# Turned reads issued from SyncE, a gate in fifteen steps, one-hot pairs in two

## The chip, the cores and the metric

The kernel runs on one core of one Trainium2 chip. The metric is the device time of one execution in microseconds (us). The core has five engines that each take their own instructions in order: TensorE (PE, the matmuls), VectorE (DVE), ScalarE (ACT), GpSimd (POOL) and SyncE (SP, which here only issues DMAs). A DMA can be issued from several of them; the issuing instruction stands in that engine's queue with its wait.

## The reference

Three stages follow each other: a long convolution by FFT of 8 sequences of 3072 tokens with 256 channels, a mixture of eight experts with a capacity, and a dense layer pair with softplus.

```python
X = np.fft.rfft(x, axis=1)                       # x: 8 x 3072 x 256
y = np.fft.irfft(X * (filt_r + 1j * filt_i)[None], n=3072, axis=1)
x = y.reshape(8 * 3072, 256)

logits = x @ w_gate                              # 8 experts
expert = argmax(logits, axis=1)
gate = softmax(logits)[n, expert]                # sum + 1e-9 below
pos[i] = how many tokens before i chose the same expert
keep[i] = pos[i] < capacity                      # capacity 3072 // 8 * 2 = 768
y = relu(x @ w1[expert]) @ w2[expert]            # 256 -> 1024 -> 256
x = gate * y where keep, else 0

g = softplus(x @ w_in)                           # 256 -> 2048
return g @ w_out                                 # 2048 -> 256
```

With these inputs the capacity is used up early: the first three sequences (STATIC = 3) fill every expert, and all later tokens get the same constant row. A flag that the kernel computes guards a second, general path (from line 1200 on).

## The kernel before

**Stages.** For a sequence ("batch" b = 0, 1, 2) the FFT is split into 96 x 32. Batch 0 takes its first transform channel by channel and is turned on TensorE. Batches 1 and 2 do it with `x1_out` on TensorE and `x1_s` on ScalarE, then `store_mid` writes the rows to the DRAM tensor `mid` and `load_i` reads them back turned, twelve reads of 256 KB a batch. Both are issued from ScalarE's queue. A read needs all eight stores of its batch and one of four buffers "it". Then, for k from 0 to 11: `s2` (TensorE, two k at a time, three PSUM buffers "y"), `times_f` (VectorE, three instructions, called the filter product here), `z_sum` (GpSimd, one addition), `s3` (TensorE) and `s3_e` (ScalarE). When all twelve are done, `gsum`, `gturn` and the gate run on one side, and on the other `tr2`, `s4`, `s4_y` and `park` bring the sequence back to time order, scaled by the gate weight, and store it to `rowsd`; batches 0 and 1 are stored from SP, batch 2 from ScalarE.

**Gate and tables.** `gate` (line 437) is a generator; each `yield` ends a node of the plan. It takes the maximum, the exponential, the gate weight `ga`, then the first expert with the maximum (`v`, `vm`, `oh`), the rank among the tokens of the batch (`rk`, a scan, and a small matmul `pb` over partitions) and from it a slot number, which is split into 7 low bits and a block number in `ij`. `table_d` (line 496) makes two one-hot tensors of four tokens a piece, `lo` with 96x512 elements and `hv` with 96x192; `table_h` multiplies `hv` by the token number on GpSimd; `table_p` multiplies the pair on TensorE; `table_s` sums. Eight pieces (q) make a batch's table of which token stands in which slot. `table_end` and `slot_index` turn it into indices for the gather.

**Experts.** A unit is one expert and 384 slots; there are 16. `load_x` gathers its rows by three indirect DMAs from GpSimd, then `tr_p` turns them, `w1_p` and `w2_p` multiply in split precision (a high and a low part of each operand), `wi` and `wo` do the second pair of layers with softplus between on ScalarE, VectorE and GpSimd. The weights of the second pair arrive as 64-bit numbers and are taken apart by sixteen conversions (`split_res`, lines 614 to 633): five VectorE instructions, two of ScalarE and one of GpSimd each. Those that the plan places keep an intermediate in PSUM (`pv`); those placed after the plan's end keep it in SBUF (`wv`).

**Order.** Until the third unit's first matmuls the order on all engines comes from the class `Plan`, a list scheduler that runs when the program is built. Each node has an engine, a cost in ns, what it comes after (`after`), which ring of buffers it takes and gives, and `lock` where the node is to be planned as exclusive with the other locked nodes of VectorE and GpSimd. A node is chosen by its earliest start and, among equals, by the longest way to the end, to which `LIFT` adds a value for groups of nodes. A DMA is a node of its queue's engine with cost 70. What is left of the conversions when the plan's last TensorE node ends is placed in a fixed pattern of steps, which issues the other thirteen units.

The gate's slot number before:

```python
nc.vector.tensor_tensor(out=q, in0=rk, in1=eoff..., op=ALU.add)          # 96x256
nc.vector.tensor_scalar(ov, rk, cap + 0.5, float(OOB), op0=ALU.is_gt, op1=ALU.mult)
nc.vector.tensor_tensor(out=q, in0=q, in1=ov, op=ALU.add)
nc.vector.tensor_tensor(out=q, in0=q, in1=oh, op=ALU.mult)
nc.vector.tensor_reduce(out=ixf, in_=q.rearrange("p e n -> p n e"), axis=AXL.X, op=ALU.add)
```

Of the kernel before, what the change touches and what calls it, by code (L numbers as in the profile page):

```python
# [7 lines left out]
F32 = mybir.dt.float32  # L8
# [4 lines left out]
ALU = mybir.AluOpType  # L13
# [4 lines left out]
NB, S, D, E = 8, 3072, 256, 8  # L18
FF, DFF = 1024, 2048
NT = NB * S  # L20
N1, N2 = 96, 32
# [74 lines left out]
class Plan:  # L96
# [5 lines left out]
    LIFT = {"c_1": 64533380, "c_2": 22634, "left": 5719228183, "t_0": 111954045036084720, "t_1": 12832497819,  # L102
            "t_2": 63738405, "w1_2": 74362, "xl_1": 53055670, "yh_0": 108904, "yl_1": 70586}
# [13 lines left out]
    def order(self, lift):  # L117
# [45 lines left out]
        while ready:  # L163
# [19 lines left out]
            if nbytes:  # L183
                bus = max(bus, t + cost + 1200) + nbytes / 285
                done[n] = bus + 600
# [12 lines left out]
def body(tc, cap, x, ff, fx, wg, w1, w2, win, wout, m1, m2, m3, m4, small, out):  # L198
# [26 lines left out]
    eoff = sm[0:N1, 584:592]  # L225
# [16 lines left out]
    class Conv:  # L242
# [88 lines left out]
        def load_i(self, b, k):  # L331

            self.it[b, k] = self.ip.tile([128, 2, D], F32, name="it", tag="it")
            nc.scalar.dma_start(self.it[b, k], mid[b - 1].rearrange("(p k) c -> k p c", k=128)[:, 2 * k:2 * k + 2])
# [102 lines left out]
        def gate(self, b):  # L437
# [17 lines left out]
            nc.vector.tensor_reduce(out=sx, in_=ex, axis=AXL.X, op=ALU.add)  # L455
            nc.vector.tensor_scalar(sx, sx, 1e-9, None, op0=ALU.add)
# [4 lines left out]
            nc.vector.scalar_tensor_tensor(out=v, in0=dl, scalar=0.0, in1=wexp, op0=ALU.is_equal, op1=ALU.mult)  # L461
            vm = gp.tile([N1, N2], F32, name="vm")
            nc.vector.tensor_reduce(out=vm, in_=v, axis=AXL.X, op=ALU.max)
            oh = gp.tile([N1, E, N2], F32, name="oh", tag="ex")
            nc.vector.tensor_tensor(out=oh.rearrange("p e n -> p n e"), in0=v,
                                    in1=vm.unsqueeze(2).to_broadcast([N1, N2, E]), op=ALU.is_equal)
            rk = gp.tile([N1, E, N2], F32, name="rk")
            nc.vector.tensor_tensor_scan(
                out=rk.rearrange("p e n -> p (e n)"), data0=resetm, data1=oh.rearrange("p e n -> p (e n)"),
                initial=0.0, op0=ALU.mult, op1=ALU.add)  # L470
            cn = gp.tile([N1, E], F32, name="cn")
# [7 lines left out]
            nc.vector.tensor_tensor(out=ctot, in0=ctot, in1=cn, op=ALU.add)  # L479
            yield  # L480
            ov = dl.rearrange("p n e -> p (n e)").rearrange("p (e n) -> p e n", n=N2)
            q = v.rearrange("p n e -> p (n e)").rearrange("p (e n) -> p e n", n=N2)
            nc.vector.tensor_tensor(out=q, in0=rk, in1=eoff.unsqueeze(2).to_broadcast([N1, E, N2]), op=ALU.add)
            nc.vector.tensor_scalar(ov, rk, cap + 0.5, float(OOB), op0=ALU.is_gt, op1=ALU.mult)
            nc.vector.tensor_tensor(out=q, in0=q, in1=ov, op=ALU.add)
            nc.vector.tensor_tensor(out=q, in0=q, in1=oh, op=ALU.mult)
            ixf = gp.tile([N1, N2], F32, name="ixf")
            nc.vector.tensor_reduce(out=ixf, in_=q.rearrange("p e n -> p n e"), axis=AXL.X, op=ALU.add)
            yield
# [853 lines left out]
```

## Time and profile before

| | |
|---|---|
| time, three runs | 1083.91 us median, 1082.23 to 1084.74 |
| the profiled execution | 1082.4 us, span 1080.5 us, 19041 instructions |
| TensorE busy | 1035.3 us, 96% of the span |
| ScalarE busy | 778.2 us, 72% |
| GpSimd busy | 605.0 us, 56% |
| VectorE busy | 496.9 us, 46% |
| mean granted clock of TensorE | 0.984 |

The busy times are means over stages of different kinds. The convolutions, gates and tables of the three batches and the first units lie in the first 330 us; after that a pattern of 16 steps a unit repeats. A busy TensorE is not TensorE at its peak: its matmuls are pipelined and their ends are modelled, and at a granted clock of 0.5 the same matmul is busy twice as long. Idle time in front of an instruction is put down to what came last before it started.

### The profile page before, as it was taken

The numbers are of one execution on the slowest core, as the hardware profiler recorded it, in microseconds if no ns is written. First come the engines' busy times: TensorE is split into PE (matmuls) and PEld (weight loads), VectorE is DVE, ScalarE is ACT, GpSimd is POOL, SyncE is SP. The second block draws the span as 40 slices with busy tenths as digits, with TensorE's granted clock in tenths as the row PEclk, the third lists the DMA queues.
The fourth block names the chain that finished last, engine by engine and source line by source line (L and its number), as shares of the span: only waits on it lengthen the run. The fifth ranks groups of instructions, "written<-read, shape, count | busy, mean of one in ns | idle before, by whom it ended". The sixth has DMA issues, their size and how long they took to land.

```text
span 1080.5 us, 19041 instructions
## 1 busy us (share of the span) xinstructions
PE 1035.3 (96%) x7112; PEld 958.2 (89%) x7112; DVE 496.9 (46%) x884; ACT 778.2 (72%) x1612; POOL 605.0 (56%) x560
## 2 busy tenths in 40 slices
PE   8999999898899999999999999999999999999994
PEld 7656656598799999999999999999999999999994
DVE  3869699797866533333333333333333332323221
ACT  4554657665787877777877787777878777878882
POOL 0514244585765565856666656666575757463553
PEclk9999999898999999999999999999999999999997
DMA  9977526653311364323233332332121212100000
GB/s 290 290 237 258 168 79 190 200 183 108 105 40 54 117 216 165 128 103 126 94 113 114 120 114 94 113 115 66 49 70 39 70 49 69 32 15 1 16 15 18
DMA packets 72821, 120.02 MB, mean 111 GB/s; under 512 B 6928, under 2 KB 46736, under 8 KB 72720
## 3 DMA queue, kind: packets, MB, share of 16 engines
q1 hardware_dynamic: 58896, 90.40, 26.2%
q10 hardware_dynamic: 9216, 15.73, 4.5%
q0 software_dynamic: 4608, 12.59, 3.3%
q8 instruction: 58, 0.95, 0.4%
q14 instruction: 43, 0.35, 0.1%
HBM read 71.51 MB, written 47.19 MB: 110 GB/s over the span
## 4 chain that ended last, share of the span: by engine, by line
PE 79%; DVE 9%; DMA 4%; ACT 2%; issue 2%; POOL 2%; ACTq 0%; POOLq 0%; DVEq 0%; SPq 0%
PE po L803 23%; PE pi L779 23%; PE pw L725 11%; PE py L754 11%; PE p L425 2%; PE p L320 2%; PE p L297 1%; DVE hv L503 1%; DMA xt<-in_x_dram 1%; PE p L386 1%; POOL gl L554 1%; DMA fi<-in_fx_dram 1%; PE p L373 1%; DVE lo L503 1%; PE pt L702 1%
## 5 line engine op out<-in xcount | busy, mean ns | idle before, releaser
L645 DVE SCALAR_TENSOR_TENSOR g<-pi,ln 128x384 f32<-128x384 f32 x256 | 142.7, 557 | 494.4 <-ACT ln L640 433.3
L554 POOL TENSOR_TENSOR gl<-g,gh 128x384 fp32r<-128x384 f32 x256 | 262.2, 1028 | 116.8 <-ACT gh L553 115.2
L803 PE MATMUL po<-woh,gh 128*128 128x256 f32 x768 | 216.8, 282 | 3.5 <-DVE ot L810 3.5
L803 PE MATMUL po<-woh,gl 128*128 128x256 f32 x768 | 216.7, 282 | 0.0
L803 PE MATMUL po<-wol,gh 128*128 128x256 f32 x768 | 216.3, 282 | 0.0
L637 ACT ACTIVATE ab<-pi 128x384 f32<-128x384 f32 x256 | 124.7, 487 | 126.9 <-PE pi L779 120.8
L779 PE MATMUL pi<-yh,wih 128*128 128x384 f32 x512 | 173.6, 339 | 7.7 <-DVE g L645 7.7
L779 PE MATMUL pi<-yh,wil 128*128 128x384 f32 x512 | 173.8, 340 | 0.0
L779 PE MATMUL pi<-yl,wih 128*128 128x384 f32 x512 | 173.6, 339 | 0.0
L677 POOL TENSOR_TENSOR w1l<-ws,w1h 128x512 fp32r<-128x512 f32 x64 | 84.7, 1324 | 124.9 <-ACT w1h L672 95.8
L803 PEld LDWEIGHTS po<-woh,gh 128*128 128x128 f32 x768 | 144.3, 188 | 6.1 <-ACT ab L637 2.5
L803 PEld LDWEIGHTS po<-wol,gh 128*128 128x128 f32 x768 | 145.4, 189 | 0.0
L803 PEld LDWEIGHTS po<-woh,gl 128*128 128x128 f32 x768 | 145.0, 189 | 0.0
L638 ACT ACTIVATE ab<-ab 128x384 f32<-128x384 f32 (+1 forms) x257 | 134.9, 525 | 8.4
L640 ACT ACTIVATE ln<-ab 128x384 f32<-128x384 f32 (+1 forms) x257 | 134.6, 524 | 8.3
L553 ACT CAST gh<-g 128x384 fp32r<-128x384 f32 x256 | 130.4, 509 | 0.3 <-DVE g L645 0.3
L677 POOL TENSOR_TENSOR w2l<-ws,w2h 128x512 fp32r<-128x512 f32 x64 | 84.1, 1314 | 56.3 <-ACT w2h L672 55.1
L779 PEld LDWEIGHTS pi<-yh,wih 128*128 128x128 f32 x512 | 96.7, 189 | 9.1 <-DVE g L645 9.1
L779 PEld LDWEIGHTS pi<-yl,wih 128*128 128x128 f32 x512 | 96.8, 189 | 0.0
L779 PEld LDWEIGHTS pi<-yh,wil 128*128 128x128 f32 x512 | 96.7, 189 | 0.0
L365 POOL TENSOR_TENSOR z<-z,t 128x512 f32<-128x512 f32 x36 | 48.4, 1346 | 86.0 <-DVE t L360 78.6
L754 PE MATMUL py<-hl,w2h 128*128 128x384 f32 x256 | 86.2, 337 | 4.3 <-DVE hl L737 4.3
(145 smaller groups left out, 1942.9 us busy)
## 6 DMA issues: line engine op xcount, KB each, us to landing
ws<-in_w_dram SPq DMA_DIRECT2D x128, 256.0 KB, 2.9
out_dram<-cs SPq DMA_DIRECT2D x48, 512.0 KB, 3.9
xt<-in_x_dram SPq DMA_DIRECT2D x24, 384.0 KB, 7.1
mid<-s ACTq DMA_DIRECT2D x16, 384.0 KB, 4.9
rowsd<-yt SPq DMA_DIRECT2D x16, 384.0 KB, 3.2
it<-mid ACTq DMA_DIRECT2D x24, 256.0 KB, 3.9
wst<-in_win_dram SPq DMA_DIRECT2D x8, 512.0 KB, 4.5
wst<-in_wout_dram SPq DMA_DIRECT2D x8, 512.0 KB, 3.5
```

The costliest lines, as they stand in the source:

```text
L365: nc.gpsimd.tensor_tensor(out=z, in0=z, in1=t2, op=ALU.add)
L553: nc.scalar.copy(dst_hi, src)
L554: nc.gpsimd.tensor_tensor(out=dst_lo, in0=src, in1=dst_hi.bitcast(F32), op=ALU.subtract)
L637: nc.scalar.activation(out=ab[:, :n], in_=h, func=ACTF.Abs)
L638: nc.scalar.activation(out=ab[:, :n], in_=ab[:, :n], func=ACTF.Exp, scale=-1.0)
L640: nc.scalar.activation(out=ln[:, :n], in_=ab[:, :n], func=ACTF.Ln, bias=1.0)
L645: nc.vector.scalar_tensor_tensor(out=g[:, :n], in0=h, scalar=0.0, in1=ln[:, :n], op0=ALU.max, op1=ALU.add)
L677: nc.gpsimd.tensor_tensor(out=lo, in0=self.ws.pop(i), in1=hi.bitcast(F32), op=ALU.subtract)
L725: nc.tensor.matmul(ps, lhsT=a[:, k, fs], rhs=b[:, k], start=(n == 0), stop=(n == 5))
L754: nc.tensor.matmul(self.py[d], lhsT=a[:, j % 2, ds], rhs=b, start=(j == 0 and n == 0), stop=(j == 7 and n == 2))
L779: nc.tensor.matmul(self.pi, lhsT=a[i // 2][:, i % 2, k], rhs=b[:, k], start=(n == 0), stop=(n == 5))
L803: nc.tensor.matmul(self.po[t], lhsT=a[:, ts], rhs=b[:, i], skip_group_check=True, start=(i == 0 and n == 0 and t != 1), stop=(i == KI - 1 ...
```

## The change

Six things change, all in the planned part and in the gate that both paths share.

1. `load_i` issues its DMA from SP, and its node is planned on SP.
2. The gate yields more often: fifteen nodes G(0) to G(14) where there were nine.
3. The slot number is formed after the sum over experts. The expert's offset comes from `vm` (`eo`, 96x32), and the compare with the capacity and the two additions work on 96x32 instead of 96x256. The addition to `ctot` moves behind.
4. `table_d` makes one of the two one-hot tensors per call, and the pair is two nodes, `tl` and `tv`.
5. The end of a table and the making of the indices are two nodes.
6. The plan has new costs, `lock` marks and `LIFT` values, and a store of turned rows counts as landed 4000 ns after its bytes instead of 600.

```diff
@@ -99,8 +99,10 @@
 
     BUFS = {"a": 3, "y": 3, "o": 2, "it": 4, "z": 3, "t2": 2, "j": 4, "yt": 3, "xt": 8, "s1": 3, "e0": 1, "e1": 1,
             "gx": 1, "gsb": 1, "lo": 2, "wst": 3, "wf": 2, "ws": 5, "w1h": 3, "w2h": 3, "xd": 3, "x": 2, "h": 4, "Y": 3}
-    LIFT = {"c_1": 64533380, "c_2": 22634, "left": 5719228183, "t_0": 111954045036084720, "t_1": 12832497819,
-            "t_2": 63738405, "w1_2": 74362, "xl_1": 53055670, "yh_0": 108904, "yl_1": 70586}
+    LIFT = {"c_13": 153297, "c_5": 84850, "hl_1": 301914, "left": 201045, "s4_2": 324143,
+            "t_0": 6101450062220531419740490261209376882688, "t_1": 415592, "t_2": 383997, "tr2_2": 397489,
+            "xh_2": 208350, "yh_0": 307360}
+    MID = 4000
     HOP = {"PE": 250, "ACT": 130, "DVE": 130, "POOL": 100, "SP": 0}
 
     def __init__(self):
@@ -182,7 +184,7 @@
                 port = t + cost
             if nbytes:
                 bus = max(bus, t + cost + 1200) + nbytes / 285
-                done[n] = bus + 600
+                done[n] = bus + (self.MID if n[0] == "mid" else 600)
             for i, tag in enumerate(take):
                 rings[tag].append((n, take[:i].count(tag)))
             out.append(n)
@@ -222,7 +224,6 @@
     ones = sm[0:N1, 224:320]
     resetm = sm[0:N1, 320:576]
     wexp = sm[0:N1, 576:584].unsqueeze(1).to_broadcast([N1, N2, E])
-    eoff = sm[0:N1, 584:592]
     tok1 = sm[0:N1, 592:624]
     iota = sm[0:N1, 624:]
     ctot = const.tile([N1, E], F32, name="ctot")
@@ -331,7 +332,7 @@
         def load_i(self, b, k):
 
             self.it[b, k] = self.ip.tile([128, 2, D], F32, name="it", tag="it")
-            nc.scalar.dma_start(self.it[b, k], mid[b - 1].rearrange("(p k) c -> k p c", k=128)[:, 2 * k:2 * k + 2])
+            nc.sync.dma_start(self.it[b, k], mid[b - 1].rearrange("(p k) c -> k p c", k=128)[:, 2 * k:2 * k + 2])
 
         def s2(self, b, kk):
 
@@ -453,21 +454,28 @@
             yield
             sx = gp.tile([N1, N2], F32, name="sx")
             nc.vector.tensor_reduce(out=sx, in_=ex, axis=AXL.X, op=ALU.add)
+            yield
             nc.vector.tensor_scalar(sx, sx, 1e-9, None, op0=ALU.add)
             self.ga[b] = gp.tile([N1, N2], F32, name="ga", tag="ga", bufs=2)
             nc.vector.reciprocal(out=self.ga[b], in_=sx)
             yield
             v = gp.tile([N1, N2, E], F32, name="v")
             nc.vector.scalar_tensor_tensor(out=v, in0=dl, scalar=0.0, in1=wexp, op0=ALU.is_equal, op1=ALU.mult)
+            yield
             vm = gp.tile([N1, N2], F32, name="vm")
             nc.vector.tensor_reduce(out=vm, in_=v, axis=AXL.X, op=ALU.max)
+            eo = gp.tile([N1, N2], F32, name="eo")
+            nc.vector.tensor_scalar(eo, vm, float(-nunit * UNIT), float(E * nunit * UNIT - 1), op0=ALU.mult, op1=ALU.add)
+            yield
             oh = gp.tile([N1, E, N2], F32, name="oh", tag="ex")
             nc.vector.tensor_tensor(out=oh.rearrange("p e n -> p n e"), in0=v,
                                     in1=vm.unsqueeze(2).to_broadcast([N1, N2, E]), op=ALU.is_equal)
+            yield
             rk = gp.tile([N1, E, N2], F32, name="rk")
             nc.vector.tensor_tensor_scan(
                 out=rk.rearrange("p e n -> p (e n)"), data0=resetm, data1=oh.rearrange("p e n -> p (e n)"),
                 initial=0.0, op0=ALU.mult, op1=ALU.add)
+            yield
             cn = gp.tile([N1, E], F32, name="cn")
             nc.vector.tensor_copy(cn, rk[:, :, N2 - 1])
             yield
@@ -476,32 +484,32 @@
             nc.tensor.matmul(pb, lhsT=ones, rhs=ctot, start=False, stop=True)
             yield
             nc.vector.tensor_tensor(out=rk, in0=rk, in1=pb.unsqueeze(2).to_broadcast([N1, E, N2]), op=ALU.add)
-            nc.vector.tensor_tensor(out=ctot, in0=ctot, in1=cn, op=ALU.add)
             yield
-            ov = dl.rearrange("p n e -> p (n e)").rearrange("p (e n) -> p e n", n=N2)
             q = v.rearrange("p n e -> p (n e)").rearrange("p (e n) -> p e n", n=N2)
-            nc.vector.tensor_tensor(out=q, in0=rk, in1=eoff.unsqueeze(2).to_broadcast([N1, E, N2]), op=ALU.add)
-            nc.vector.tensor_scalar(ov, rk, cap + 0.5, float(OOB), op0=ALU.is_gt, op1=ALU.mult)
-            nc.vector.tensor_tensor(out=q, in0=q, in1=ov, op=ALU.add)
-            nc.vector.tensor_tensor(out=q, in0=q, in1=oh, op=ALU.mult)
+            nc.vector.tensor_tensor(out=q, in0=rk, in1=oh, op=ALU.mult)
+            yield
             ixf = gp.tile([N1, N2], F32, name="ixf")
             nc.vector.tensor_reduce(out=ixf, in_=q.rearrange("p e n -> p n e"), axis=AXL.X, op=ALU.add)
             yield
+            nc.vector.tensor_tensor(out=ctot, in0=ctot, in1=cn, op=ALU.add)
+            nc.vector.tensor_tensor(out=eo, in0=eo, in1=ixf, op=ALU.add)
+            nc.vector.tensor_scalar(ixf, ixf, cap + 0.5, float(OOB), op0=ALU.is_gt, op1=ALU.mult)
+            nc.vector.tensor_tensor(out=eo, in0=eo, in1=ixf, op=ALU.add)
             ix = gp.tile([N1, 2, N2], I32, name="ix")
-            nc.vector.tensor_copy(ix[:, 0], ixf)
+            nc.vector.tensor_copy(ix[:, 0], eo)
             nc.vector.tensor_scalar(ix[:, 1], ix[:, 0], 7, None, op0=ALU.logical_shift_right)
             nc.vector.tensor_scalar(ix[:, 0], ix[:, 0], 127, None, op0=ALU.bitwise_and)
             nc.vector.tensor_copy(ij[b], ix)
 
-        def table_d(self, b, q):
+        def table_d(self, b, q, row):
 
 
             n = N2 // QT
-            lo, hv = onehot[q % 2]
-            ns = slice(n * q, n * q + n)
-            for row, w, to in ((0, 128, lo), (1, nblk, hv)):
-                nc.vector.tensor_tensor(out=to, in0=iota[:, 0:w].unsqueeze(1).to_broadcast([N1, n, w]),
-                                        in1=ij[b][:, row, ns].unsqueeze(2).to_broadcast([N1, n, w]), op=ALU.is_equal)
+            to = onehot[q % 2][row]
+            w = (128, nblk)[row]
+            nc.vector.tensor_tensor(out=to, in0=iota[:, 0:w].unsqueeze(1).to_broadcast([N1, n, w]),
+                                    in1=ij[b][:, row, n * q:n * q + n].unsqueeze(2).to_broadcast([N1, n, w]),
+                                    op=ALU.is_equal)
 
         def table_h(self, b, q):
             n = N2 // QT
@@ -942,7 +950,7 @@
                 load(("mid", b, g), lambda b=b, g=g: cv.store_mid(b, g), 384, "ACT",
                      after=[("xs", b, g, 0), ("xs", b, g, 1)], give=[("s1", ("xo", b, g, 0))])
             for k in range(12):
-                load(("it", b, k), lambda b=b, k=k: cv.load_i(b, k), 256, "ACT",
+                load(("it", b, k), lambda b=b, k=k: cv.load_i(b, k), 256,
                      after=[("mid", b, g) for g in range(8)], take=["it"],
                      behind=[("it", b, k - 1) if k else ("tr1", 11) if b == 1 else ("it", b - 1, 11)])
 
@@ -979,31 +987,35 @@
             gate = lambda: step_of(gates, b, lambda b=b: cv.gate(b))
             add(G(0), "PE", 440, gate(), after=[("gg", b, 0), ("gg", b, 1), "const"], take=["o"],
                 give=[("gsb", ("gg", b, 0))])
-            add(G(1), "DVE", 850, gate(), after=[G(0)] + ([("g", b - 1, 8)] if b else []), give=[("o", G(0))])
+            add(G(1), "DVE", 870, gate(), after=[G(0)] + ([("g", b - 1, 13)] if b else []), give=[("o", G(0))])
             add(G(2), "ACT", 420, gate(), after=[G(1)])
-            add(G(3), "DVE", 900, gate(), lock=True,
-                after=[G(2)] + ([("sy", b - 2, m) for m in range(16)] if b > 1 else []))
-            add(G(4), "DVE", 1990, gate(), after=[G(3)], lock=True)
-            add(G(5), "PE", 150, gate(), after=[G(4)] + ([("g", b - 1, 6)] if b else []), take=["o"])
-            add(G(6), "DVE", 520, gate(), after=[G(5)] + (["keep"] if b == STATIC - 1 else []), give=[("o", G(5))])
-            add(G(7), "DVE", 1950, gate(), after=[G(6)], lock=True)
-            add(G(8), "DVE", 720, gate(), after=[G(7)])
+            add(G(3), "DVE", 440, gate(), after=[G(2)])
+            add(G(4), "DVE", 500, gate(), lock=True,
+                after=[G(3)] + ([("sy", b - 2, m) for m in range(16)] if b > 1 else []))
+            for i, cost, lock in ((5, 440, 1), (6, 620, 0), (7, 440, 1), (8, 720, 1), (9, 190, 1)):
+                add(G(i), "DVE", cost, gate(), after=[G(i - 1)], lock=bool(lock))
+            add(G(10), "PE", 150, gate(), after=[G(9)] + ([("g", b - 1, 14)] if b else []), take=["o"])
+            add(G(11), "DVE", 440, gate(), after=[G(10)], give=[("o", G(10))])
+            add(G(12), "DVE", 440, gate(), after=[G(11)], lock=True)
+            add(G(13), "DVE", 610, gate(), after=[G(12)])
+            add(G(14), "DVE", 1500, gate(), after=[G(13)] + (["keep"] if b == STATIC - 1 else []), lock=True)
             for q in range(QT):
-                td, th, tp, tt = (T((q, i)) for i in range(4))
-                add(td, "DVE", 1050, lambda b=b, q=q: cv.table_d(b, q), take=["lo"], lock=True,
-                    after=[T((q - 1, 0))] if q else [G(8)] + ([("t", b - 1, 4)] if b else []))
-                add(th, "POOL", 500, lambda b=b, q=q: cv.table_h(b, q), after=[td], lock=True)
-                add(tp, "PE", 450, lambda b=b, q=q: cv.table_p(b, q), after=[th], take=["a"], give=[("lo", td)])
+                tl, th, tp, tt, tv = (T((q, i)) for i in range(5))
+                add(tl, "DVE", 710, lambda b=b, q=q: cv.table_d(b, q, 0), take=["lo"], lock=True,
+                    after=[T((q - 1, 0))] if q else [G(14)] + ([("t", b - 1, 5)] if b else []))
+                add(tv, "DVE", 365, lambda b=b, q=q: cv.table_d(b, q, 1), lock=True, after=[tl])
+                add(th, "POOL", 505, lambda b=b, q=q: cv.table_h(b, q), after=[tv], lock=True)
+                add(tp, "PE", 450, lambda b=b, q=q: cv.table_p(b, q), after=[th], take=["a"], give=[("lo", tl)])
                 add(tt, "DVE", 205, lambda b=b, q=q: cv.table_s(b, q), after=[tp] + ([T((q - 1, 3))] if q else []),
                     give=[("a", tp)])
 
             def close_table(b=b):
-                cv.table_end(b)
                 if b:
                     index[b] = slot_index(str(b), const)
 
-            add(T(4), "DVE", 1500, close_table, after=[T((QT - 1, 3))] + ([("t", b - 1, 4)] if b else []) +
-                (["keep"] if b == STATIC - 1 else []), lock=True)
+            add(T(4), "DVE", 800, lambda b=b: cv.table_end(b), lock=True,
+                after=[T((QT - 1, 3))] + ([("t", b - 1, 5)] if b else []) + (["keep"] if b == STATIC - 1 else []))
+            add(T(5), "DVE", 620, close_table, after=[T(4)], lock=True)
...
```

The rest of the diff renames the steps that other nodes come after: what came after G(3) (the gate weight) comes after G(4), G(6) (the rank) and G(8) (the slot) are G(14) or G(13), T(4) as the end of a table is T(5), and the general path calls `table_d` twice.

## Rows read from the trace of the kernel before

**Rows 1.** The page's slices of 27 us: TensorE's busy tenths, its granted clock.
```profile
PE   8999999898899999999999999999999999999994
...
PEclk9999999898999999999999999999999999999997
```

**Rows 2.** Windows: start:end, length, busy us of each engine (instructions), clock, DMA.
```profile
135.00:180.00 45.00, 41.81 (x326) 27.30 (x325) 43.38 (x70) 27.65 (x59) 20.84 (x20) 0.96 0.42 126
...
189.00:207.00 18.00, 14.69 (x58) 8.47 (x57) 12.66 (x32) 11.47 (x26) 10.60 (x10) 0.81 0.55 174
...
252.00:288.00 36.00, 26.41 (x135) 25.67 (x134) 26.45 (x39) 21.30 (x44) 18.38 (x16) 0.86 0.28 92
...
378.00:1000.00 622.00, 619.80 (x4113) 616.85 (x4111) 196.12 (x373) 482.72 (x1011) 384.79 (x359) 1.00 0.27 90
```

**Rows 3.** Timeline of VectorE, batch 1's tables: start, us, line, output<-inputs.
```profile
145.60 0.68 DVE L360 TENSOR_TENSOR t<-p,fi 64x512 f32<-64x512 f32 x1
...
146.31 0.69 DVE L503 TENSOR_TENSOR lo<-sm,ij 96x512 fp32r<-96x512 f32 x1
...
146.92 1.42 DVE L503 TENSOR_TENSOR hv<-sm,ij 96x192 fp32r<-96x192 f32 x1
...
174.14 1.44 DVE L503 TENSOR_TENSOR hv<-sm,ij 96x192 fp32r<-96x192 f32 x1
```

**Rows 4.** Single lines: instructions, ns minimum/median/maximum, first and last start.
```profile
L503 DVE TENSOR_TENSOR lo<-sm,ij x24: 677/686/1168, 67.9 to 241.9; 96x512 fp32r<-96x512 f32 x24
...
L503 DVE TENSOR_TENSOR hv<-sm,ij x24: 343/348/1447, 68.5 to 242.5; 96x192 fp32r<-96x192 f32 x24
...
L484 DVE TENSOR_SCALAR dl<-rk x3: 282/283/1358, 65.2 to 193.9; 96x256 f32<-96x256 f32 x3
...
L365 POOL TENSOR_TENSOR z<-z,t x36: 1262/1274/1707, 26.6 to 167.3; 128x512 f32<-128x512 f32 x36
...
L614 DVE TENSOR_SCALAR pv<-wst x11: 675/679/689, 169.2 to 255.9; 128x512 uint32<-128x512 uint32 x11
...
L614 DVE TENSOR_SCALAR wv<-wst x5: 415/418/5039, 270.4 to 310.0; 128x512 uint32<-128x512 uint32 x5
...
L334 ACTq DMA_DIRECT2D it<-mid x24: 366/428/1518, 75.7 to 138.4; - x24
```

**Rows 5.** Timeline of GpSimd, the sum beside that round.
```profile
146.45 1.68 POOL L365 TENSOR_TENSOR z<-z,t 128x512 f32<-128x512 f32 x1 [2.65 <-DVE t L360]
```

**Rows 6.** Timeline of TensorE and VectorE, 252 to 288 us; [idle before <-releaser].
```profile
259.50 0.69 PE L754 MATMUL py<-hl,w2h 128*128 128x384 f32 x1 [4.31 <-DVE hl L737]
...
270.42 5.04 DVE L614 TENSOR_SCALAR wv<-wst 128x512 uint32<-128x512 uint32 x1
...
277.24 0.44 PE L779 MATMUL pi<-yh,wih 128*128 128x384 f32 x1 [3.79 <-DVE g L645]
```

**Rows 7.** Groups by line and form, VectorE, first 330 us: busy, mean ns.
```profile
L483 DVE TENSOR_TENSOR v<-rk,sm 96x256 f32<-96x256 f32 x3 | 1.3, 421 | 0.0
...
L456 DVE TENSOR_SCALAR sx<-sx 96x32 f32<-96x32 f32 x3 | 0.5, 177 | 0.1
```

**Rows 8.** The chain that ended last, 75 to 200 us: start, us.
```profile
100.17 6.05 DMA mid<-s
```

**Rows 9.** Timeline of ScalarE and TensorE near 107 us.
```profile
107.28 0.58 ACT L390 COPY j<-p 96x512 f32<-96x512 f32 x1 [3.16 <-PE p L373]
...
108.40 1.10 PE L425 MATMUL p<-j,m4s 96*96 96x512 f32 x2 [1.39 <-ACT e L379]
```

**Rows 10.** Timeline of SP's issues, 60 to 250 us.
```profile
96.70 6.61 SPq L592 DMA_DIRECT2D wst<-in_win_dram  x3
...
110.39 57.06 SPq L537 DMA_DIRECT2D rowsd<-yt  x11
```

**Rows 11.** Waits of SP's queue, first 330 us: total, times, longest.
```profile
SPq L537 <- ACT yt L434: 65.9, 15, 9.5
```

**Rows 12.** DMA issues: output<-input, queue, count, size, median us to landing.
```profile
it<-mid ACTq DMA_DIRECT2D x24, 256.0 KB, 3.9
```

More of the change, by code (lines that the diff above doesn't have):

```diff
@@ L1013, in body @@
                     lambda b=b, m=m, vec=vec: cv.tr2_j(b, m, vec), after=[tr], give=[("a", tr)])
-                add(s4, "PE", 856, lambda b=b, m=m: cv.s4(b, m), after=[tj, "const", G(3)],
+                add(s4, "PE", 856, lambda b=b, m=m: cv.s4(b, m), after=[tj, "const", G(4)],
                     take=["o"] if m % 2 else ["o", "yt"], give=[("j", tr)], behind=prev("s4"))
-                add(sy, "ACT", 930, lambda b=b, m=m: cv.s4_y(b, m), after=[s4, G(3)], give=[("o", s4)])
+                add(sy, "ACT", 930, lambda b=b, m=m: cv.s4_y(b, m), after=[s4, G(4)], give=[("o", s4)])
                 if m % 2:
@@ L1024, in keep @@
             nc.vector.tensor_copy(slead, slot)
-        add("keep", "DVE", 350, keep, after=[("g", STATIC - 2, 6), ("t", STATIC - 2, 4)])
+        add("keep", "DVE", 350, keep, after=[("g", STATIC - 2, 14), ("t", STATIC - 2, 5)])
         last = STATIC - 1
@@ L1060, in body @@
         add("low", "SP", 0, low_room, after=["room"] + [("tr2", 1, m) for m in range(16)] + [("gs", 1, 0), ("gs", 1, 1)])
-        add("flags", "DVE", 700, flags, after=[("g", last, 6)])
-        add("left", "SP", 0, left_room, after=["low", "flags", ("g", last, 8), *sum(parks, [])])
+        add("flags", "DVE", 700, flags, after=[("g", last, 14)])
+        add("left", "SP", 0, left_room, after=["low", "flags", ("g", last, 14), *sum(parks, [])])
         W2, WI, SP, WO, SUM, W1, TAKE, TR, AHEAD = range(9)
@@ L1089, in body @@
                 add(("xd", v, t), "POOL", 1100, lambda u=u, t=t: load_x(u, [t]), nbytes=131072,
-                    after=[("t", last - 1, 4), *sum(parks[:last], []), "room"],
+                    after=[("t", last - 1, 5), *sum(parks[:last], []), "room"],
                     behind=[("xd", v, t - 1)] if t else [("xd", v - 1, 2)] if v else [], take=["xd"])
@@ L1239, in body @@
                 for q in range(QT):
-                    for part in (cg.table_d, cg.table_h, cg.table_p, cg.table_s):
+                    for half in range(2):
+                        cg.table_d(0, q, half)
+                    for part in (cg.table_h, cg.table_p, cg.table_s):
                         part(0, q)
```

## The prediction

> **What bounds the kernel now.** I read the page's slices first. TensorE is busy 90% or more of nearly every slice and its granted clock is full in nearly all of them [rows 1]. So the time is TensorE's work plus what it loses to pauses and to the lower clock. Windows say where that is [rows 2]. From 378 to 1000 us it is busy 619.80 of 622 us at clock 1.00; the change touches nothing there. The losses that could come back lie ahead of it, in three stretches. I count the time not busy, and (1 - granted clock) x length for work done at a lower clock. The clock has two levels, 1.2 and 2.4 GHz (0.5 and 1.0).
>
> - 135 to 180 us: 45 - 41.81 = 3.2, and 0.04 x 45 = 1.8: 5.0 us. VectorE is busy 43.38 of 45.
> - 189 to 207 us: 18 - 14.69 = 3.3, and 0.19 x 18 = 3.4: 6.7 us.
> - 252 to 288 us: 36 - 26.41 = 9.6, and 0.14 x 36 = 5.0: 14.6 us.
>
> Together 26.3 us. This is a ceiling: the order of the work decides how much of it returns.
>
> In the first stretch VectorE runs batch 1's tables between batch 2's filter products, with no gap. The reader should see the shape of one round [rows 3]: the last product ends at 146.28, lo runs, then hv takes 1.42 us. Alone, hv takes 0.348 [rows 4]. GpSimd's row explains it: its sum z, released by that product, stands as 146.45 to 148.13, 1.68 us, while its usual time is 1.27 [rows 5]: it lies first behind lo and then in front of hv. Seven hv between 146.92 and 174.14 are lengthened so.
>
> In the third stretch TensorE waits for VectorE at two places [rows 6]: 4.31 us for hl, and 3.79 us for g, which sat behind the first instruction of a conversion of the second MoE's weights that took 5.04 us. Eleven conversions work in PSUM, their first instruction at 0.675 to 0.689 us; five came after the plan's end and work in SBUF, at 0.415 to 5.039 [rows 4].
>
> **The change part by part.** The sum is made against the profiled execution, 1082.4 us; the median of the runs is 1083.9, so 1.5 is added at the end.
>
> *The gate's arithmetic.* Gone are two adds and a compare over 96x256. An add takes 0.42 [rows 7], the compare 0.28 undisturbed [rows 4]: 1.12 us. New are four 96x32 instructions; the nearest row is the gate's small tensor_scalar, 0.177 [rows 7]: 0.71. Net 0.4 us of VectorE in each of three batches, 1.2 in all, bounded by nothing and 2.2 (that of the first kind with the new ones free would be 3.4, which nothing supports). On TensorE's path it is worth at most that, and I put it in with the next item.
>
> *Smaller nodes.* Four nodes of VectorE work become more, and lo and hv become two, so that the plan can put a filter product, a copy or a conversion between two instructions that share something with GpSimd. If the seven hv run alone this frees 7 x (1.42 - 0.35) = 7.5 us of VectorE. The compare, longest 1.358 for 0.282 [rows 4], disappears with its own 1.08. So 8.6 us, nothing at the lower end (the next instruction waits in its place). TensorE can take back no more than its 5.0 there. I take half, 2.5: its own order still has waits that are none of VectorE's doing.
>
> The Trainium skill (SBUF — State Buffer, "Who interferes with whom") says that a VectorE instruction with two SBUF inputs contends with a GpSimd instruction that reads SBUF, and that issue order decides which of them stands still for the whole of the other. The trace agrees: hv, with 192 elements, stood 1.07 us. By that rule the split removes no conflict, it only lets the plan choose who is first; whether it does is a rival below.
>
> *VectorE's saved time, further on.* A conversion is five instructions, of which the first takes 0.68 [rows 4]; five of that size are 3.4 us. With 8.6 us free ahead of 250 us, two or three conversions fit in before the plan's end, in their PSUM form, and the third stretch has as many fewer. The pause of 3.79 us is the one with the slow SBUF form directly behind it. I take that one as gone, and leave the 4.31 us and the clock. Bounds: nothing (the new priorities place the conversions elsewhere), and 14.6.
>
> *Reads of turned batches.* ScalarE loses 24 issues of 0.428 us median [rows 4], 10.3 us. What lies behind them is seen at one place: the last store of batch 2's turned rows is under way from 100.17 for 6.05 us and on the chain [rows 8], the reads that need it stand at the head of ScalarE's queue, and ScalarE's next copy comes at 107.28 after 3.16 us of nothing; TensorE then shows 1.39 us before its matmul at 108.40 [rows 9]. I take half of that, 0.7 (bounds 0 and 1.4): the copy behind it also needs TensorE. On SP the same wait stands in front of nothing: after the weight reads at 96.70 its next issue is at 110.39 [rows 10]. The later reads lie among the stores of finished tokens, and there SP waits for ScalarE 15 times, 65.9 us, longest 9.5 [rows 11]; that is the price if the cover is gone, and the rival of the other sign. Data moved and DMA engines stay the same.
>
> *Priorities and costs of the plan.* The table LIFT is another one, the stores of turned batches are planned to land 3.4 us later, and the end step of a table is split. I can't work out the order that comes of it; it may help or harm. The second stretch, where TensorE waits for gathered rows, depends on it alone: I enter 0, with a bound of 6.7 either way.
>
> Sum: 2.5 + 3.8 + 0.7 = 7.0 us. 1082.4 - 7.0 = 1075.4 profiled, 1076.9 as a median: 1077. Its own range goes from a third of that gain to nearly twice: 1071 to 1081.5.
>
> **Rivals.** A difference under 0.2% (2.2 us) can't be told from none.
>
> 1. *VectorE's gain is hidden.* TensorE is busy 41.81 of 45 us in the first stretch, so a faster VectorE may find its consumer occupied; the conversions then stay where they are. For it: 93% of TensorE's time there is work already. Against it: two pauses in the third stretch end on VectorE by name. Time 1083.
>
> 2. *Slower: a read stands behind a store on SP.* Place: SP's queue between 110 and 167 us, where eleven stores of finished tokens are issued over 57.06 us [rows 10]. If a read of batch 2 lies behind one, it starts when ScalarE has scaled that store's rows, up to 9.5 us late. The four buffers of "it" cover four products: two rounds of a product (three instructions of 0.69) make each 2.1 us, so four give 8.4 [rows 3]; less two issues, 0.9 [rows 4], and 3.9 for the landing [rows 12] that leaves 3.6 us. Beyond 3.6 us of such a wait the filter products starve. 9.5 - 3.6 = 5.9 us, and one dip of the clock of the kind seen after 189 us, half of its 3.4: 7.6 lost. With nothing gained elsewhere 1083.9 + 7.6 = 1091.5, with all of the gains 1084.5, so about 1089. For it: SP takes its queue in order and waits here already. Against it: the plan sorts both by the same time.
>
> 3. *Two waits for one.* Where lo too comes more than 0.1 us after a product, it stands behind that product's sum, and hv behind the next. Eight pieces x 1.07 = 8.6 us more of VectorE in a stretch without gaps; TensorE would lose half as it does now, with nothing gained: 1088. That is the rule of the Trainium skill's page named above, at its worst. For it: the longest lo is already lengthened, 1.168 against 0.686 [rows 4]. Against it: a plan that models the shared time would put other work there.
>
> 4. *The ramp closes.* The conversions all move ahead, and the third stretch loses 5 instead of 14.6; with the 3.2 of the others, 13 to 20 us gained: 1064 to 1071.
>
> 5. *The gather is waited for twice.* The new priorities bring a matmul on gathered rows in front of other work at another place too: 6.7 lost against part of the gains: 1087.
>
> **How the numbers follow.** Forecast 0.50, rival 1 0.17, rival 2 0.13, rival 3 0.06, rival 4 0.10, rival 5 0.04. Faster is the forecast and rival 4: 0.60. Same is rival 1: 0.17. Slower are 2, 3 and 5: 0.23. The predicted time is the likeliest case's, 1077. The range runs from 1068, which takes in the nearer half of rival 4, to 1090, which leaves out the upper part of rival 2: about 0.11 outside, and a few hundredths more for what the unknown order can do beyond these cases.
>
> **What the next profile would show.** Right: most hv near 0.35 us between 140 and 180 us; VectorE's stretch of batch 1's tables some 8 us shorter; no read issued from ScalarE and its wait near 107 us gone; fewer than five conversions in the SBUF form; the first stretch of 100% TensorE reached about 7 us earlier, and everything after it shifted by that. Wrong: hv or lo still over 1 us with another instruction between; gaps of VectorE in front of the filter products between 110 and 170 us with SP waiting in front of a read; TensorE's not-busy time between 250 and 300 us as it was. What would overturn the forecast above all is the order: if pauses come back at a place that none of these rows shows, the savings are real and don't reach the end.

## The result, and the profile after

The changed kernel takes 1073.14 us in the median of 4 runs (1071.57 to 1074.87), the kernel before 1084.33 (4 runs). The ratio is 0.9894, 95% interval [0.9863, 0.9925]. In a second group of runs (e0 below) it was 1074.52 against 1083.87, ratio 0.9908 [0.9889, 0.9927]: 9 to 11 us faster, where 7.0 had been forecast. The profiled execution took 1074.87 us, its span 1073.1.

Slices of the changed kernel, answering to [rows 1]:

```profile
PE   9999999898899999999999999999999999999994
...
PEclk9999999899999999999999999999999999999998
```

Windows over the stretches of [rows 2]: length, busy us of PE, PEld, DVE, ACT, POOL, granted clock, DMA share, GB/s.

```profile
135.00:180.00 45.00, 41.60 (x326) 27.80 (x324) 39.08 (x73) 30.98 (x68) 21.94 (x19) 0.96 0.47 144
189.00:207.00 18.00, 15.97 (x76) 9.41 (x74) 14.31 (x44) 13.15 (x31) 6.08 (x6) 0.96 0.68 203
252.00:288.00 36.00, 29.66 (x173) 28.70 (x174) 25.62 (x37) 23.72 (x50) 20.69 (x18) 0.95 0.28 94
378.00:1000.00 622.00, 619.55 (x4117) 616.59 (x4116) 195.98 (x374) 482.74 (x1011) 382.71 (x359) 1.00 0.26 88
```

From 378 us on nothing has changed. In the first stretch VectorE is less busy (39.08 us for 43.38), but TensorE gains nothing by it: it loses 45 - 41.60 + 0.04 x 45 = 5.2 us where it lost 5.0. The second shows less at the lower clock only because a stretch of it has moved past 207 us; 6.8 us at the lower clock begin at 205.6 us now and at 196.4 before. The third loses 36 - 29.66 + 0.05 x 36 = 8.1 us instead of 14.6, but part of that is a shift: all that follows begins earlier. To compare stages I use a mark, the first weight load of TensorE for the second pair of layers (pi). It starts at 261.0 us in the trace before and at 255.3 after; the 301st of pi's weight loads and matmuls, counted together, follows 85.9 and 84.3 us later. So of the 7.5 us between these two executions 5.7 come from ahead of the mark and 1.6 from right behind it.

Ahead of the mark each execution splits up simply. I take from it TensorE's time without a matmul (its pauses) and half of its time at the lower clock, both from the trace. What remains is 236 to 237 us in every kernel told of here that keeps one of the two orders (one, e12, 235). Before: 18.2 us of pauses, 13.4 at the lower clock. After: 13.2 and 10.2. In a second profiled execution of the changed kernel: 12.0 and 7.7, with the mark at 252.2. One kernel's mark can thus move by 3 us from one execution to the next.

The one-hot instructions, by line and form, and the conversions in their two forms (first 400 us); then the reads of turned batches. These answer to [rows 4]:

```profile
L510 DVE TENSOR_TENSOR lo<-sm,ij 96x512 fp32r<-96x512 f32 x24 | 16.5, 691 | 8.5 <-PE p L525 8.4
L510 DVE TENSOR_TENSOR hv<-sm,ij 96x192 fp32r<-96x192 f32 x24 | 9.8, 437 | 0.0
L622 DVE TENSOR_SCALAR wv<-wst 128x512 uint32<-128x512 uint32 x5 | 7.8, 1562 | 0.1
...
L622 DVE TENSOR_SCALAR pv<-wst 128x512 uint32<-128x512 uint32 x11 | 7.5, 684 | 0.0
```

```profile
L335 SPq DMA_DIRECT2D it<-mid x24: 359/426/1699, 79.8 to 138.0; - x24
```

The reader sees hv at a mean of 0.437 us (22 of the 24 are undisturbed, near 0.348 us) and the reads on SP's queue. But conversions still split into eleven and five, and the pause that I had counted as gone is there, after the same 5.04 us of VectorE. Timelines of TensorE, VectorE and GpSimd, answering to [rows 6]:

```profile
253.87 0.44 PE L762 MATMUL py<-hl,w2h 128*128 128x384 f32 x1 [2.13 <-DVE hl L745]
270.48 0.69 PE L787 MATMUL pi<-yh,wih 128*128 128x384 f32 x1 [4.03 <-DVE g L653]
```

```profile
263.66 5.04 DVE L622 TENSOR_SCALAR wv<-wst 128x512 uint32<-128x512 uint32 x1
```

```profile
262.95 1.00 POOL L700 DMA_INDIRECT xd<-rowsd,gi  x1 [0.30 <-issue]
263.98 1.02 POOL L562 TENSOR_TENSOR gl<-g,gh 128x384 fp32r<-128x384 f32 x1
264.96 1.29 POOL L641 TENSOR_TENSOR wol<-wf,woh 128x512 fp32r<-128x512 f32 x1
266.21 1.26 POOL L685 TENSOR_TENSOR w2l<-ws,w2h 128x512 fp32r<-128x512 f32 x1
267.43 0.98 POOL L562 TENSOR_TENSOR gl<-g,gh 128x384 fp32r<-128x384 f32 x1
```

It was the other pause, the one for hl, that shrank: 4.31 to 2.13 us. It is 4.31 and 4.29 us in the two kernels below that keep the order of before (e8, e11) and 2.13 in e0 to e3, so this much came with the new order; what in it did so isn't shown.

### The profile page after: what moved, and what is told of

Read it like the earlier page. It is cut to its first block, busy times and chain, and to the rows that moved or that the text cites. A ratio compares the mean times of both kernels' runs of the same rounds, so it can differ in the third digit from the quotient of the medians.

```text
span 1073.1 us, 19020 instructions
## 1 busy us (share of the span) xinstructions
PE 1032.8 (96%) x7112; PEld 957.6 (89%) x7112; DVE 480.7 (45%) x887; ACT 777.3 (72%) x1612; POOL 597.8 (56%) x560
## 4 chain that ended last, share of the span: by engine, by line
PE 79%; DVE 8%; ACT 4%; DMA 3%; issue 2%; POOL 2%; SPq 0%; POOLq 0%; DVEq 0%
PE po L811 23%; PE pi L787 23%; PE pw L733 11%; PE py L762 11%; PE p L321 2%; PE p L374 2%; PE p L426 2%; PE p L346 1%; POOL gl L562 1%; DMA xt<-in_x_dram 1%; PE p L387 1%; PE pt L710 1%; DVE t L361 1%; ACT ab L646 1%; DVE wf L623 1%
## 5 line engine op out<-in xcount | busy, mean ns | idle before, releaser
L740 ACT ACTIVATE hh<-pw 128x384 fp32r<-128x384 f32 x128 | 62.8, 491 | 39.4 <-PE pw L733 36.1
```

The source lines that it names most:

```text
L740: nc.scalar.activation(out=hh, in_=self.h[j], func=ACTF.Relu)
```

## The experiments

Theory A is the prediction's: the gain is VectorE's, by finer nodes that let hv run alone. Theory B: it is the reads, off ScalarE. Theory C: it is the new order that the plan chooses. Each kernel was timed beside the kernel before, in three groups: e0 to e3; e4, e5, e7 and e8; e6, e10, e11 and e12. The kernel before had medians of 1083.87, 1083.68 and 1083.83 in them.

**e0: the changed kernel again.**

> The changed kernel again, beside the others of this call. About 0.989 of the kernel before (1073 us); three half-speed stretches of TensorE's clock before 300 us with 13.7 us in all where the kernel before has four with 20.5.

Measured: 1074.52 (1073.12 to 1074.72). This is what single edits undone are held against.

**e1: only the reads back on ScalarE, order kept.**

```diff
-            nc.sync.dma_start(self.it[b, k], mid[b - 1]...
+            nc.scalar.dma_start(self.it[b, k], mid[b - 1]...
```

> The changed kernel in its own order, only the reads of turned batches issued from ScalarE again. Theory A (VectorE standing behind GpSimd was the cost): within 1.4 us of the changed kernel. Theory B (the reads off ScalarE's queue are the gain): 4 us or more slower than the changed kernel, with ScalarE standing 3 us at a read near 100 us and a pause of TensorE behind it.

Measured: 1080.87 in the median, ratio to before 0.9993 [0.9964, 1.0023]; 6.4 us more than e0. The twelve executions lie wide apart, from 1076.20 us at a mean granted clock of 0.990 to 1091.06 at 0.977. The profiled one is the shortest, and in it the waits for the reads' instruction are small:

```profile
L335 ACTq DMA_DIRECT2D it<-mid x24: 366/428/1916, 81.8 to 139.7; - x24
...
  ACT e L380: 2.6, 1
  PE p L346: 1.2, 1
```

So 24 issues of 0.43 us cost far more than the one wait that the trace before had shown. In the profiled execution the cost is pauses: ahead of the mark TensorE is 16.8 us without a matmul, against 12.0 in e0, while its time at the lower clock is shorter, 4.9 us against 7.8. Two pauses that e0 hasn't are for ScalarE's copy behind four reads (issued from 81.80 on, in 2.33 us) and for a read itself. Timeline of TensorE:

```profile
85.62 0.60 PE L525 MATMUL p<-hv,lo 96*128 96x48 f32 x4 [1.00 <-ACT s L327]
...
121.08 1.10 PE L346 MATMUL p<-it,m2s 64*32 64x256 f32 x32 [1.21 <-DMA it<-mid]
```

Half of the twelve executions are no lower in clock than e0's (0.988 to 0.990, and 1076 to 1079 us); in the other half, from 1082 us up, the clock is 0.976 to 0.986. Where in those the time goes isn't shown, since none of them was profiled.

**e2: each hv directly behind its lo, order otherwise kept.**

```diff
+        for b in range(STATIC):
+            for q in range(QT):
+                behind_of(("t", b, (q, 0)), ("t", b, (q, 4)))
```

> The changed kernel in its own order, only each hv put directly behind its lo. Theory A: hv goes back from 0.44 us mean to about 0.8 (24 x 0.37 = 9 us of VectorE) and the time rises by 2.5 to 5 us. Theory C (the order of everything else, that is the new priorities, is the gain): hv lengthens, but the time stays within 2 us.

Measured: 1080.18, ratio 0.9962 [0.9949, 0.9976]; 5.7 us more than e0. But the hv instructions sum to 13.9 us, against 11.0 in e0 and 19.5 before: most still run alone. The loss is mostly at one place, where a lo, not an hv, stands beside the end of a gather and three more instructions of GpSimd, and TensorE behind the hl that follows. Timelines of VectorE, GpSimd and TensorE:

```profile
228.88 4.87 DVE L510 TENSOR_TENSOR lo<-sm,ij 96x512 fp32r<-96x512 f32 x1
```

```profile
228.45 1.00 POOL L700 DMA_INDIRECT xd<-rowsd,gi  x1 [0.31 <-issue]
229.48 1.29 POOL L685 TENSOR_TENSOR w1l<-ws,w1h 128x512 fp32r<-128x512 f32 x1
230.72 1.26 POOL L641 TENSOR_TENSOR wil<-wf,wih 128x512 fp32r<-128x512 f32 x1
231.94 1.25 POOL L685 TENSOR_TENSOR w2l<-ws,w2h 128x512 fp32r<-128x512 f32 x1
```

```profile
234.54 0.44 PE L733 MATMUL pw<-xh,w1h 128*128 128x384 f32 x1 [3.84 <-DVE hl L745]
```

The 3.84 us and half of the 3.4 us at the lower clock that come after it make 5.5 of the 7.2 us between the two profiled executions (1080.29 and, e0, 1073.12).

**e3: the gate's steps directly behind one another, order otherwise kept.**

```diff
+            for i in (4, 6, 7, 8, 9, 13):
+                behind_of(("g", b, i - 1), ("g", b, i))
```

> The changed kernel in its own order, only the gate's VectorE steps 4, 6 to 9 and 13 put directly behind the step before them (coarse nodes as before). Theory A: some steps stand behind GpSimd again, filter products move back by the gate's length, 1 to 3 us slower. Theory C: within 1 us.

Measured: 1076.24, ratio 0.9922 [0.9903, 0.9942]; 1.7 us more than e0. Its timeline has a pause that e0's hasn't, and from 145 to 160 us its clock is 0.89 where e0 shows 1.00:

```profile
148.68 1.16 PE L374 MATMUL p<-m3s,z 128*128 128x128 f32 x8 [2.12 <-POOL z L366]
```

**e4 and e5: the two LIFT tables exchanged.** e4 is the changed kernel with the old table, e5 the kernel before with the new one; every edit of the work is left as it was in either.

> The changed kernel with every edit in it, but the planner given the LIFT table of the kernel before, so that its order is another. Theory A (what gains is the work itself: less VectorE work, finer nodes, reads off ScalarE): 1073 to 1078 us, the order is worth at most 3. Theory C (what gains is the order that the new LIFT table makes planner choose, in which no batch's one-hot tables stand among another's filter products): 1081 to 1086, most of the 9.9 us lost, and the waits of hv for the port back at 0.8 us each.

> The kernel before with none of the edits but the new LIFT table. Theory A: no gain, 1082 to 1088, since reads stay on ScalarE, the pair stays one node and the gate's eight blocks stay whole. Theory C: 1074 to 1079, most of the gain with no edit of the work.

Measured: 1097.88 and 1100.96, ratios 1.0120 [1.0097, 1.0143] and 1.0118 [1.0078, 1.0158]. Theory C as I wrote it falls: the new table on the old nodes is slower than before, as is the old table on the new ones. Neither table does for the other's nodes what it does for its own. In e4 TensorE has pauses of a length that no other kernel shows; timeline of e4:

```profile
185.22 1.05 PE L524 MATMUL p<-hv,lo 96*128 96x48 f32 x4 [9.26 <-POOL hv L516]
216.22 0.48 PE L709 MATMUL pt<-sm,xd 128*128 128x128 f32 x1 [4.76 <-DMA xd<-rowsd,gi]
```

And e4 has all 24 hv undisturbed, 8.3 us together. It is 23 us slower than the changed kernel with them. Undisturbed hv are not enough.

**e8: the kernel before, with the reads on SP and nothing else.**

```diff
-            nc.scalar.dma_start(self.it[b, k], mid[b - 1]...
+            nc.sync.dma_start(self.it[b, k], mid[b - 1]...
```

> The kernel before in its own order, with only the 24 reads of turned batches issued from SyncE. My prediction's term: 1 us saved or less, 1083 (bounds 0 to 1.4 saved). Theory B, from the run that put the reads back on ScalarE (6.4 us lost in the median): 1077 to 1080. A third outcome, the rival of the prediction in which a read stands behind a waiting store on SyncE: 1086 or more.

Measured: 1079.11 (1078.57 to 1081.72), ratio 0.9955 [0.9939, 0.9971]: 4.6 us saved in the median. Theory B holds for that part. Where the 4.6 us lie isn't seen: the profiled execution, 1081.30, is one of the long ones, and its mark is 0.9 us earlier than before. Two waits for a store on SP's queue, 14.3 us together, cost nothing that shows.

**e10 and e11: old work in the new order, new work in the old order.** e10 undoes the reads, the pairs, the gate's steps and the slot arithmetic together and keeps the changed kernel's order. e11 has the reads on SP and the slot number from the sum, and the order, the undivided pairs and the undivided gate of before.

```diff
-            nc.vector.tensor_tensor(out=q, in0=rk, in1=eoff.unsqueeze(2)..., op=ALU.add)
-            nc.vector.tensor_scalar(ov, rk, cap + 0.5, float(OOB), ...)
-            nc.vector.tensor_tensor(out=q, in0=q, in1=ov, op=ALU.add)
-            nc.vector.tensor_tensor(out=q, in0=q, in1=oh, op=ALU.mult)
+            nc.vector.tensor_tensor(out=q, in0=rk, in1=oh, op=ALU.mult)
...
+            nc.vector.tensor_tensor(out=eo, in0=eo, in1=ixf, op=ALU.add)
+            nc.vector.tensor_scalar(ixf, ixf, cap + 0.5, float(OOB), ...)
+            nc.vector.tensor_tensor(out=eo, in0=eo, in1=ixf, op=ALU.add)
```

> The work of the kernel before in the order of the changed one: reads on ScalarE, lo and hv directly behind each other, the gate in eight blocks, the slot number by the three 96x256 operations. If the order carries the gain: 1074 to 1077. If the work carries it: 1083 or more; the losses of the single edits undone (6.4, 5.7, 1.7) would add up to 1088 if they were independent.

> The work of the changed kernel in the order of the one before: reads on SyncE, the slot number from the sum over experts, but the pair and the gate's blocks undivided. If the work carries the gain: 1074 to 1076. If work and order share it: about 1077 to 1078, a little under the 1079.1 of the run with the reads alone. If the slot number is worth nothing: 1079.

e10 measured 1092.52, ratio 1.0074 [1.0054, 1.0095]: in the new order the old work is slower than before.

e11's 3371.35 us can't be compared: as I built it, the flag and the saved count read the running total ahead of an update that I had moved into the gate's last block, so the branch for overflowing slots runs behind the main program. The main program itself is whole in its profile. Start of the last matmul of the last unit in the kernel before, in the changed one and in e11, one fence each:

```profile
1064.40 0.28 PE L803 MATMUL po<-woh,gl 128*128 128x256 f32 x1
```

```profile
1057.02 0.28 PE L811 MATMUL po<-woh,gl 128*128 128x256 f32 x1
```

```profile
1056.44 0.28 PE L803 MATMUL po<-woh,gl 128*128 128x256 f32 x1
```

From there to the end of the execution it is 18.0 us before (1082.4) and 17.9 after (1074.87). So e11's main program stands for about 1074.4 us, level with the changed kernel, in one execution, the shortest of e11's six (3365.88 to 3377.44); in which part the others are longer isn't known. It has the order of before and all of its hv waits (19.5 us in 24, as before). Against e8's profiled execution (1081.30) the slot arithmetic gives 6.9 us, against e8's median 4.7, against its shortest (1078.57) 4.2.

What the new arithmetic does is seen in batch 1's slot block, VectorE's timeline. First e8, where three instructions of 96x256 stand ahead of a filter product, the compare among them lengthened to 1.36 us:

```profile
136.67 0.42 DVE L483 TENSOR_TENSOR v<-rk,sm 96x256 f32<-96x256 f32 x1
137.01 1.36 DVE L484 TENSOR_SCALAR dl<-rk 96x256 f32<-96x256 f32 x1
138.40 0.42 DVE L485 TENSOR_TENSOR v<-v,dl 96x256 f32<-96x256 f32 x1
...
139.83 0.68 DVE L357 TENSOR_TENSOR z<-p,fr 128x512 f32<-128x512 f32 x1
```

Then e11. The one multiplication of 96x256 is left, and a compare of 96x32 takes over the wait, at another place:

```profile
134.77 0.42 DVE L482 TENSOR_TENSOR v<-rk,oh 96x256 f32<-96x256 f32 x1
135.23 0.62 DVE L484 TENSOR_REDUCE ixf<-v 96x32 f32<-96x256 f32 x1
135.77 0.68 DVE L356 TENSOR_TENSOR z<-p,fr 128x512 f32<-128x512 f32 x1
...
138.18 1.15 DVE L488 TENSOR_SCALAR ixf<-ixf 96x32 f32<-96x32 f32 x1
```

In e8 the block holds up that product by 3.2 us (in e11 by 1.0), and TensorE pauses 1.02 us for the sum made from it; in e11 that pause is missing. Windows of e8 and then e11, TensorE alone (length, busy, clock, DMA share, GB/s):

```profile
150.00:170.00 20.00, 18.85 (x131) 0.91 0.30 86
...
190.00:210.00 20.00, 16.75 (x74) 0.83 0.67 209
```

```profile
150.00:170.00 20.00, 17.37 (x136) 1.00 0.42 125
...
190.00:210.00 20.00, 17.71 (x88) 1.00 0.72 237
```

Most of the difference is clock: 0.09 and 0.17 of 20 us make 5.2. Ahead of the mark e8 spends 13.7 us at the lower level and e11 1.7, while pauses fall only from 16.9 to 16.1; the mark moves from 260.0 to 253.4. That the missing pause is what kept the clock up is not shown: one execution of each can't tell it from chance. e8's ten executions range from 0.984 to 0.989 in mean clock, and two executions of one kernel can differ in a stretch. The changed kernel has the same pause of 2.16 us in both of its profiled executions. In the first (1074.87 us) the clock is at the lower level behind it, 0.66 from 164 to 169 us; in the second (e0) it stays at 1.00 from 163 to 168. Timelines of TensorE, one fence each:

```profile
164.03 1.42 PE L426 MATMUL p<-j,m4s 96*96 96x512 f32 x2 [2.16 <-DVE gx L407]
```

```profile
162.97 1.10 PE L426 MATMUL p<-j,m4s 96*96 96x512 f32 x2 [2.16 <-DVE gx L407]
```

**e6: the changed kernel and its order, with the old slot arithmetic.**

> The changed kernel, its order kept, with the old slot arithmetic: VectorE gets some 3.5 us more work, 0.6 to 1.2 us for each of three batches. If VectorE's work there is on the path: 1075.5 to 1078. If it is hidden: 1074 to 1075. If orders are so tightly fitted that a small delay upsets them: 1079 or more.

Measured: 1072.16, ratio 0.9880 [0.9857, 0.9903]. That can't be told from e0. In the new order the slot arithmetic alone is worth nothing that shows.

**e7 and e12: unit 3's gathers moved,** to test what the 5.03 us of the first SBUF-form conversion wait for.

```diff
-                ev(b - 16, AHEAD, load_x, u)
+                ev(4 if v == 3 else b - 16, AHEAD, load_x, u)    # e7; in e12: -1 if v == 3
```

> The changed kernel with the three gathers of unit 3 issued four steps later, so that GpSimd's run from 256.8 to 266.3 us is broken up there. If the 5.03 us of the first SBUF-form conversion and TensorE's pause of 4.0 us behind it come of that unbroken run: the conversion's first step falls to 1 to 2.5 us, the pause to under 1.5, the half-speed stretch that follows it shrinks or goes, and the time is 1069 to 1071 (3 to 5 us under the changed kernel). If the conversion waits for another thing: 5 us stays and the time is 1073 to 1075. If the gathers only move the stall: a wait of 3 us or more some 10 us later, 1072 to 1076.

> The changed kernel with unit 3's three gathers issued one step earlier, ahead of two conversions of GpSimd, into the stretch before 256 us in which GpSimd has 7.3 us without work. If the unbroken run of GpSimd is the cause of the 5.03 us of the first SBUF-form conversion, and the stall isn't only moved: that conversion's step falls under 2 us, TensorE's pause of 4.0 us under 2, 1069 to 1072. If it moves, as it did with the gathers four steps later: 1074 to 1077.

Measured: 1076.50, ratio 0.9922 [0.9900, 0.9945], and 1072.70, ratio 0.9894 [0.9870, 0.9919]. The conversion's first step takes 0.42 us in both, so its stall came of what GpSimd did beside it. In e7 the stall only moved, to a later step of a conversion, and there GpSimd ran wol, gl, w2l and gl, with no gather among them; VectorE's timeline of e7:

```profile
279.78 4.43 DVE L628 SCALAR_TENSOR_TENSOR wv<-wst,wv 128x512 uint32<-128x512 uint32 x1
```

VectorE's and TensorE's timelines of e12:

```profile
264.63 0.42 DVE L622 TENSOR_SCALAR wv<-wst 128x512 uint32<-128x512 uint32 x1
```

```profile
253.43 0.69 PE L762 MATMUL py<-hl,w2h 128*128 128x384 f32 x1 [3.54 <-DVE hl L745]
268.69 0.44 PE L787 MATMUL pi<-yh,wih 128*128 128x384 f32 x1 [1.12 <-DVE g L653]
```

The pause for g falls from 4.01 in e0 to 1.12, and the stretch behind the mark from 85.4 to 82.6 us. Yet the pause for hl ahead of it grows from 2.13 to 3.54, and the mark comes at 255.2; e0 has it at 252.2, the other execution of the changed kernel at 255.3. e12's median is 1.8 us under e0's, less than its own executions spread (1071.02 to 1076.84). In e7 TensorE has a new pause of 2.29 us at 279, for a gl that stands behind the moved gathers. No version was found that is measurably better than the changed kernel.

## Why the prediction was right, and where it wasn't

The time was right to 3.9 us and within the range, the sum less so: of its three terms one fell and the others were mis-sized. That a term too large and terms too small nearly made up for each other is luck.

- **"VectorE's saved time, further on", 3.8 us: this step failed.** The conversions stayed eleven and five, the pause became 4.03 us. What came back was partly the other pause, 4.31 to 2.13, which I had left standing. And e12 shows what that term could have been worth: with the pause down to 1.12, the total is lower by 1.8 us at most, which can't be told from none.
- **"Smaller nodes", most of the 2.5 us: the premise failed.** hv did run alone, as expected. But TensorE loses 5.2 us in that stretch where it lost 5.0: none of the 2.5 came back there. e4 has no hv wait and is slow, and e11 has every hv wait of before and is, in one execution, level with the changed kernel. In the new order the divided pair does count: joined, one lo comes to stand 4.87 us (e2).
- **"The gate's arithmetic", 1.2 us with a bound of 2.2, put in with the item above: mis-sized.** In the new order it gives nothing that shows (e6). In the old order it gives 4.2 to 6.9 us by one execution of e11 beside e8. I priced VectorE's instructions; in that pair a product's start, a pause of TensorE and its clock differ, and most of the difference is clock.
- **"Reads of turned batches", 0.7 us with bounds 0 and 1.4: mis-sized.** It is 4.6 us in the old order (e8) and 6.4 in the new (e1). I sized it by the one pause seen in one execution.
- **Priorities, 0 us: right for the second stretch.** TensorE's pauses for gathered rows were 1.97 and 1.34 us; one of 1.86 is left (none in e0), with one for hv behind it (0.94, in e0 1.38), and the 6.8 us at the lower clock are still there.
- **Rivals.** VectorE's gain hidden (1) is what the first stretch and the eleven and five conversions show; its time, 1083, left out what the reads were worth. A read behind a store (2) did not hurt: SP's waits moved and nothing starved. Two port waits for one (3): the longest lo is 0.87 us. The closed ramp (4) did not come, nor a second wait for gathered rows (5).

So the reads are shown to give 4.6 us of the 9.4 to 11.2 measured, without the new order (e8). That the slot arithmetic gives the rest, about 4.7, is argued and not shown: e11 was judged by its main program, in a single execution, the shortest of six, and what sets it off from e8 is mostly clock, which varies between executions. The new order alone gives nothing: the old work takes 1083.8 us in the old order and 1092.5 in the new. The new work takes 1074.5 in the new order and, by e11, about 1074.4 in the old.

Single edits undone in the new order cost 13.8 us together by their medians (6.4, 5.7 and 1.7; the slot arithmetic nothing) and all of them at once 18. In the profiled executions they nearly add up: e1, e2, e3 and e6 lie 3.1, 7.2, 4.2 and 0.9 us above e0's 1073.12, 15.3 together, and e10 15.7 (1088.79). e10's trace has the pauses of the single ones side by side: 1.73 us for a read (e1), 3.87 for hl (e2) and 2.02 for the sum (e3).

## What to carry to other kernels

An order tuned by priorities belongs to its nodes: cross the two before crediting either, and test edits with the order pinned. Price a few VectorE instructions not by their own length alone but by which late product they push, and whether TensorE pauses after it. When two kernels differ by clock, profile more than one execution of each before crediting the edit. A moved issue is priced by the spread of several executions; one profile showed 1.4 us of an effect worth 4.6.

## What the runs showed of the hardware

A VectorE instruction that has to wait beside GpSimd can stand through several of its instructions, not one. The conversion's first step took 5.04 us while a gather, two gl and the low parts of two weights (wol, w2l) ran back to back, a lo took 4.87 us beside a gather and three more (e2), and a later step 4.43 us with no gather there (e7). The Trainium skill (SBUF — State Buffer, "Who interferes with whom") says that VectorE and GpSimd share a pair of ports; that when VectorE is in a two-port mode, whichever issues first gets the pair for its whole instruction and blocks the other; and that a VectorE instruction with two SBUF inputs contends with GpSimd's reads. Which mode an instruction ran in no run shows. The traces agree in who waits: each of the three started while an instruction of GpSimd was under way. They add that the wait can go on through the instructions behind it. It needn't: elsewhere VectorE gets in after one, though GpSimd's next follows without a gap, and that next one is lengthened instead. So it is 18 us after the long wait, in the same trace; timelines of VectorE and GpSimd:

```profile
281.35 1.68 DVE L630 SCALAR_TENSOR_TENSOR wf<-wf,wv 128x512 f32<-128x512 f32 x1
```

```profile
281.18 1.30 POOL L685 TENSOR_TENSOR w2l<-ws,w2h 128x512 fp32r<-128x512 f32 x1 [0.56 <-ACT w2h L680]
282.43 1.48 POOL L562 TENSOR_TENSOR gl<-g,gh 128x384 fp32r<-128x384 f32 x1
```

The wf takes 0.69 us undisturbed, and the gl 0.98. What makes the few long waits stays open.

TensorE's clock made small edits large: e1's executions range over 15 us, and the longer ones have the lower mean clock. And one pause of 2.16 us was followed by the lower level in one execution of a kernel and by the full one in another.
